# Reordering the opening of an attention + mixer kernel: earlier loads, decay rows moved on chip, the first batch ahead of the mixers

## Chip, cores, metric

One core of a Trainium2 chip. The metric is device time of one execution in microseconds (us), lower is better; medians over several executions are given. TensorE (PE in the profile) multiplies, ACT (ScalarE) does exponentials and copies, VectorE (DVE) copies and masks, GpSimd (POOL) issues most loads, SyncE (SP) the others.

Two words are used throughout. The *opening* is what happens before channel mixing of the first token group starts; the *dense part* is everything after that.

## The reference

```python
# q, k, v: (8 batches, 8 heads, 576, 64); s: (8, 8, 576)
scores = q @ k.T / sqrt(64)
cum    = cumsum(max(s, 0))
scores = where(causal, -1e9, scores + min(-(cum[:, None] - cum[None, :]), 0))
x      = softmax(scores) @ v                    # heads side by side: (8, 576, 512)
u      = x + (x.T @ U @ V).T                    # sequence mixing, rank 32
out    = u + relu(u @ w_ch1) @ w_ch2            # channel mixing, 512 -> 2048 -> 512
```

## The kernel before

Attention goes by pairs of heads, four pairs per batch, 32 in all. One pair is three generators: `transposes` (TensorE turns q and k, VectorE copies them into a slot, and the decay rows, that is the cumulative sums in parts, are added to the slot by DMA), `scores` (matmuls of 68 rows, exponentials on ACT, masking on VectorE) and `values`. After each batch comes `seqmix`, then one group of 512 tokens of `chanmix` is queued as *filler*: each `yield` of the attention lets the filler do one step (four matmuls of 512 columns).

```python
    # ... decay rows: computed on VectorE for all heads, written to HBM
    nc.sync.dma_start(out=rows_hbm.rearrange("r n c s -> n r c s"), in_=rows)
    # ... identity, masks, memsets on POOL, then the loads, all issued by POOL:
    load_qk(0, 4)                  # q, k of batch 0 in four pieces each
    load_v(0)

    def transposes(n):
        b, hp = divmod(n, PB)      # PB = 4 pairs per batch
        slot = slots[n % NSLOT]
        nc.sync.dma_start(out=slot[D:KA, :, 0 : 2 * S],
                          in_=rows_hbm[:, ds(2 * n, 2)].rearrange("r n c s -> r n (c s)"))
        for hh in range(2):
            ...                    # 8 transposes on TensorE, 2 copies on VectorE
            yield                  # 2 yields;  scores: 4 yields, values: 2 yields

    def chanmix(g):                # 32 yields in all
        for nf in range(NF):       # 16 steps, 4 matmuls each
            ...
            yield
        for i in range(4):         # 16 steps, 4 matmuls each
            ...

    fill = []
    def step_fill():
        while fill:
            if next(fill[0], fill) is not fill:
                return
            fill.pop(0)

    def run(gen):
        for _ in gen:
            step_fill()

    drain(transposes(0))
    load_weights()                 # U, V, w1, w2: 8 MB read, 4 MB in bf16
    for n in range(NP + 1):        # NP = 32 pairs
        b, hp = divmod(n, PB)
        if hp == 0 and b + 1 < B:
            load_qk(b + 1, 1)
            load_v(b + 1)
        if n + 1 < NP:
            run(transposes(n + 1))
        if n < NP:
            run(scores(n))
        if n > 0:
            run(values(n - 1))
            if n % PB == 0:
                run(seqmix(b - 1))
                fill.append(chanmix(b - 1))
```

The softmax here doesn't subtract the row's maximum and nothing guards it: scores larger than these inputs give would overflow.

## Time and profile before

| | us |
|---|---|
| time, median (range) | 430.1 (429.5 to 431.3) |
| span of the profiled execution | 429.4 |
| first score matmul | 25.0 |
| sequence mixing of batch 0 starts | 64.2 |
| first channel-mixing matmul of group 0 / of group 1 | 69.9 / 112.4 |

This is the busy time by stretch. The columns are the stretch in us, its length, then busy us (and instructions) of PE, PE weight loads, DVE, ACT, POOL, then the granted clock, the DMA share (the time of all packets over that of 16 engines, so it can exceed 1) and GB/s.

```profile
20.00:30.00 10.00, 4.86 (x44) 3.75 (x45) 1.10 (x4) 3.64 (x8) 7.47 (x9) 1.00 1.74 182
30.00:40.00 10.00, 10.00 (x116) 8.48 (x115) 9.82 (x22) 7.39 (x16) 0.70 (x1) 1.00 1.17 206
40.00:50.00 10.00, 1.14 (x10) 0.58 (x8) 1.23 (x4) 2.46 (x6) 0.83 (x1) 0.68 1.64 191
50.00:60.00 10.00, 6.96 (x92) 6.03 (x93) 5.80 (x10) 1.68 (x4) 3.49 (x4) 0.50 3.26 107
...
70.00:80.00 10.00, 10.00 (x94) 5.43 (x93) 6.80 (x12) 5.38 (x9) 3.48 (x5) 1.00 2.28 71
```

TensorE is the limit from 70 us on (10.00 of 10 us), and it is idle for most of 40 to 50 us. The clock column of the first 40 us is not to be trusted: the durations there are those of half rate (the prediction explains how to see it).

These are TensorE's waits in the first 70 us (what it waited for, total us, times, longest):

```profile
PE pwork L173 <- DMA q_sd<-in_q_dram: 18.4, 3, 9.1
PE pscore L193 <- DMA slot_121<-rows_hbm: 9.8, 1, 9.8
PE pwork L173 <- DMA k_sd<-in_k_dram: 5.2, 3, 1.9
```

18.4 us went into waiting for q, 9.8 for the decay rows of pair 0 that came back from HBM, 5.2 for k. And this is the timeline of TensorE just before sequence mixing of batch 0 (start, duration, line, output and operands, count). Slots go round in threes, so slot_122 and slot_123 here are pairs 4 and 5, which belong to batch 1:

```profile
57.14 1.51 PE L193 MATMUL pscore<-slot_122 68*128 68x128 bf16 x9 [0.75 <-DVE slot_122 L178]
...
59.29 1.52 PE L193 MATMUL pscore<-slot_122 68*128 68x128 bf16 x9
...
61.45 2.91 PE L193 MATMUL pscore<-slot_123 68*128 68x128 bf16 x18
64.16 2.34 PE L269 MATMUL pwork<-x_sb,U_sb 128*128 128x512 bf16 x5
```

### The profile page before, as it was taken

To read this page: it belongs to the slowest core of one execution; us is meant where nothing else is said; L and a number is where in the kernel's file an instruction comes from. 1 tells how busy PE (TensorE), PEld (TensorE's weight loads), DVE (VectorE), ACT (ScalarE), POOL (GpSimd) and SP (SyncE) were. 2 spreads that over 40 slices of the span, in tenths; PEclk is the share of its full clock that TensorE was granted. 3 is DMA by queue.
4 is the path that set the end of the run, shared out by engine and by line. 5 is a ranking of instruction groups with operands and counts; after the bars stand their busy time and mean duration, and the time that the engine had idled before them with its cause. 6 is when DMAs were issued, how large, how long until landed. Compare 5 with 4: busy or idle time off the path is not lost.

```text
span 429.4 us, 8600 instructions
## 1 busy us (share of the span) xinstructions
PE 390.8 (91%) x3608; PEld 229.5 (53%) x3608; DVE 232.9 (54%) x451; ACT 191.4 (45%) x369; POOL 60.4 (14%) x83
## 2 busy tenths in 40 slices
PE   0168289999999999999999999999999999999996
PEld 0156265556555655555565555655565565444443
DVE  7538186566856675567556755685667535101001
ACT  1057053743475347534753375337533760440620
POOL 9750134100310031003100310000000000000000
PEclk9999558999999999999999999999999999999999
DMA  3999999841944193419351925100010001101001
GB/s 53 179 194 206 164 106 125 70 82 52 79 59 84 53 82 51 90 52 81 44 100 52 81 38 103 54 26 4 21 58 27 2 3 49 49 2 73 25 26 73
DMA packets 59351, 29.76 MB, mean 69 GB/s; under 512 B 42320, under 2 KB 53616, under 8 KB 59312
## 3 DMA queue, kind: packets, MB, share of 16 engines
q0 software_dynamic: 53392, 18.44, 51.5%
q1 hardware_dynamic: 5920, 10.77, 7.1%
q8 instruction: 28, 0.46, 0.5%
q14 instruction: 11, 0.09, 0.1%
HBM read 37.58 MB, written 10.03 MB: 111 GB/s over the span
## 4 chain that ended last, share of the span: by engine, by line
PE 85%; DMA 9%; POOL 3%; DVE 1%; issue 1%; POOLq 0%
PE pwork L331 29%; PE pwork L344 29%; PE pscore L193 10%; DMA k_sd<-in_k_dram 7%; PE pwork L246 6%; PE pwork L173 3%; PE pwork L269 2%; DMA v_slot_91<-in_v_dram 2%; PE pwork L355 2%; PE pwork L282 2%; PE pwork L290 2%; POOL k_sd L112 1%; POOL v_slot_91 L120 1%; POOL q_sd L112 1%; DVE uT L298 0%
## 5 line engine op out<-in xcount | busy, mean ns | idle before, releaser
L344 PE MATMUL pwork<-w_sb,hT 128*128 128x512 bf16 x576 | 143.8, 379 | 0.0
L331 PE MATMUL pwork<-uT,w_sb 128*128 128x512 bf16 x576 | 140.5, 379 | 0.2 <-DVE uT L298 0.2
L338 ACT ACTIVATE hT<-pwork 128x512 bf16<-128x512 f32 x144 | 87.6, 608 | 77.8 <-PE pwork L331 77.3
L331 PEld LDWEIGHTS <-w_sb 128*128 128x128 bf16 x576 | 51.1, 98 | 46.9 <-issue 0.3
L344 PEld LDWEIGHTS <-hT 128*128 128x128 bf16 x576 | 50.2, 98 | 42.6
L364 DVE COPY o_sb<-pwork 128x512 f32<-128x512 f32 x36 | 24.9, 692 | 71.1 <-PE pwork L355 71.1
L204 ACT ACTIVATE pT_127<-pscore 128x512 bf16<-128x512 f32 x32 | 19.3, 602 | 74.9 <-PE pscore L193 74.9
L255 DVE RECIPROCAL rec<-pwork 128x5 f32<-128x5 f32 x64 | 12.1, 193 | 60.8 <-PE pwork L246 60.6
L204 ACT ACTIVATE pT_128<-pscore 128x512 bf16<-128x512 f32 x32 | 19.1, 597 | 53.1 <-PE pscore L193 53.0
L178 DVE COPY slot_122<-pwork 64x576 bf16<-64x576 bf16 x44 | 35.2, 800 | 5.4 <-PE pwork L173 4.7
L178 DVE COPY slot_121<-pwork 64x576 bf16<-64x576 bf16 x44 | 35.1, 799 | 3.2 <-PE pwork L173 2.5
L173 PE MATMUL pwork<-identity,q_sd 72*128 72x72 bf16 x256 | 19.9, 206 | 18.6 <-DMA q_sd<-in_q_dram 18.4
L193 PE MATMUL pscore<-slot_121 68*128 68x128 bf16 (+4 forms) x198 | 24.5, 255 | 9.9 <-DMA slot_121<-rows_hbm 9.8
L178 DVE COPY slot_123<-pwork 64x576 bf16<-64x576 bf16 x40 | 32.0, 801 | 2.3 <-PE pwork L173 1.6
L173 PEld LDWEIGHTS <-q_sd 72*128 72x128 bf16 x256 | 16.8, 104 | 29.5 <-DMA q_sd<-in_q_dram 18.8
L256 DVE TENSOR_TENSOR x_sb<-pwork,rec 128x320 bf16<-128x320 f32 x64 | 31.2, 491 | 2.0
L205 DVE TENSOR_TENSOR pT_127<-pT_127,keep 128x512 bf16<-128x512 bf16 x32 | 13.1, 413 | 25.9 <-ACT pT_127 L204 25.9
L193 PE MATMUL pscore<-slot_122 68*128 68x128 bf16 (+4 forms) x198 | 25.3, 259 | 0.9 <-DVE slot_122 L178 0.7
L193 PEld LDWEIGHTS <-slot_121 68*128 68x128 bf16 x198 | 15.4, 104 | 19.3 <-issue 10.8
L173 PE MATMUL pwork<-identity,k_sd 72*128 72x72 bf16 x256 | 19.6, 208 | 5.2 <-DMA k_sd<-in_k_dram 5.2
L246 PEld LDWEIGHTS <-pT_127 128*128 128x128 bf16 x480 | 20.5, 102 | 6.9 <-issue 0.2
L246 PEld LDWEIGHTS <-pT_128 128*128 128x128 bf16 x480 | 20.4, 102 | 7.0
(79 smaller groups left out, 399.0 us busy)
## 6 DMA issues: line engine op xcount, KB each, us to landing
out_dram<-o_sb SPq DMA_DIRECT2D x36, 256.0 KB
w_sb<-in_moe_w_ch_dram POOLq DMA_DIRECT2D x2, 2048.0 KB, 19.8
q_sd<-in_q_dram POOLq DMA_DIRECT2D x7, 576.0 KB, 7.6
k_sd<-in_k_dram POOLq DMA_DIRECT2D x7, 576.0 KB, 10.7
v_slot_91<-in_v_dram POOLq DMA_DIRECT2D x12, 128.0 KB, 8.1
v_slot_94<-in_v_dram POOLq DMA_DIRECT2D x12, 128.0 KB, 5.7
v_slot_97<-in_v_dram POOLq DMA_DIRECT2D x8, 128.0 KB, 9.1
q_sd<-in_q_dram POOLq DMA_DIRECT2D x4, 144.0 KB, 5.1
```

The costliest lines, as they stand in the source:

```text
L173: nc.tensor.transpose(tp[:, c, t2, :], src[:, h, ds(t2 * 128, 128)], identity[:TP, :TP])
L178: nc.vector.tensor_copy(dst[:, :, :, :, par], tp[par * D : par * D + D].rearrange("p c t m -> p c m t"),)
L193: nc.tensor.matmul(dst, lhsT=kT[:, ds(j * 128, 128)], rhs=qT[:, lo:hi], start=True, stop=True,)
L204: nc.scalar.activation(pT[:, hh, 0:512], diag, EXP, scale=scale)
L205: nc.vector.tensor_tensor(pT[:, hh, 0:512], pT[:, hh, 0:512], keep.rearrange("p a b -> p (a b)"), op=ALU.min)
L246: nc.tensor.matmul(po[:, i, :], lhsT=pT[:, hh, ds(place(j, i), 128)], rhs=vt[:, j, h, :], start=(j == 0), stop=(j == i), skip_group_check= ...
L255: nc.vector.reciprocal(rec, po[:, :, D : D + 1])
L256: nc.vector.tensor_tensor(x_sb[:, :, ds(h * D, D)], po[:, :, 0:D], rec.to_broadcast([128, 5, D]), op=ALU.mult,)
L331: nc.tensor.matmul(f1, lhsT=w1_sb[:, kt, ds(nf * 128, 128)], rhs=uT[:, kt, ds(g * 512, 512)], start=(kt == 0), stop=(kt == 3),)
L338: nc.scalar.activation(hT[:, nf, :], f1, RELU)
L344: nc.tensor.matmul(f2, lhsT=hT[:, nf, ds(i * 128, 128)], rhs=w2_sb[:, nf, :], start=(nf == 0), stop=False, skip_group_check=True,)
L364: nc.vector.tensor_copy(o_sb, f2)
```

## The change

Its intent: issue the first loads at once; move the decay rows of batch 0 inside SBUF and send only those of the other batches through HBM; finish attention of batch 0 before any mixing; put q and k of batch 1 between the two weight matrices; keep TensorE's clock up with filler matmuls. The core of the diff:

```diff
-    load_qk(0, 4)                                # behind memsets, in the middle of the setup
+    alloc_qk(0)
+    load_qk(0, 0, 2)                             # first thing on POOL
     identity = consts.tile([128, 128], BF16)
     make_identity(nc, identity)
+    load_qk(0, 2, 2)
+    load_qk(0, 4, 4)
 ...
+    for n in range(PB):                          # rows of batch 0: SBUF to SBUF
+        for hh in range(2):
+            nc.sync.dma_start(
+                out=slots[n][D:KA, hh, 0 : 2 * S],
+                in_=rows[2 * n + hh : 2 * n + hh + 1].rearrange("n r c s -> n r (c s)"),
+            )
 ...
+    nc.gpsimd.dma_start(out=w1_sb, in_=...)      # weights around q, k of batch 1
+    alloc_qk(1)
+    load_qk(1, 0, H)
+    nc.gpsimd.dma_start(out=w2_sb, in_=...)
+    load_v(1)
 ...
-    NSLOT = 3
+    NSLOT = 5
-                nc.vector.tensor_copy(           # slot copies
+                copy = nc.scalar.copy if n < 2 else nc.vector.tensor_copy
 ...
-    drain(transposes(0))
-    load_weights()
-    for n in range(NP + 1):
+    spin(8)                                      # useless 512-column matmuls
+    for n in range(PB):
+        for _ in transposes(n):
+            spin(1)
+    for n in range(PB):
+        drain(scores(n))
+        if n > 0:
+            drain(values(n - 1))
+    drain(values(PB - 1))
+    drain(seqmix(0))
+    fill.append(chanmix(0))
+    fill_with(4)                                 # four filler steps at once
+    run(transposes(PB))
+    for n in range(PB, NP + 1):
         ...
-        if n > 0:
+        if n > PB:
             run(values(n - 1))
```

Memsets also moved from POOL to VectorE, and one decay row is computed on ACT.

More of the change, by code (lines that the diff above doesn't have):

```diff
@@ L59, in pwork, with alloc_qk, load_qk @@
         return ps_w.tile([128, 512], FP32, tag="w", name="pwork")
-    early = work.tile([128, NF, 512], BF16, tag="hT", name="hT").rearrange("p a b -> p (a b)")
-    s_sb = early[:BH, 8 * S : 10 * S].bitcast(FP32)
+    s_early = work.tile([128, NF, 512], BF16, tag="hT", name="hT").rearrange("p a b -> p (a b)")
+    s_sb = s_early[:BH, 8 * S : 10 * S].bitcast(FP32)
+    cum = s_early[:BH, 10 * S : 12 * S].bitcast(FP32)
+    rows = s_early[:BH, : 8 * S].rearrange("p (r c s) -> p r c s", r=4, c=2)
     nc.sync.dma_start(out=s_sb, in_=s.rearrange("b h s -> (b h) s"))
-    nc.vector.tensor_scalar(s_sb, s_sb, 0.0, 1.0 / scale, op0=ALU.max, op1=ALU.mult)
-    cum = early[:BH, 10 * S : 12 * S].bitcast(FP32)
-    nc.vector.tensor_tensor_scan(cum, s_sb, s_sb, 0.0, op0=ALU.add, op1=ALU.max)
-    rows = early[:BH, : 8 * S].rearrange("p (r c s) -> p r c s", r=4, c=2)
-    nc.gpsimd.memset(rows[:, 0:3, 0, :], 1.0)
-    nc.gpsimd.memset(rows[:, 3, 1, :], 1.0)
-    rest = s_sb
-    nc.vector.tensor_scalar_mul(rows[:, 3, 0, :], cum, -1.0)
-    nc.vector.tensor_copy(rows[:, 0, 1, :], cum)
-    nc.vector.tensor_sub(rest, cum, rows[:, 0, 1, :])
-    nc.vector.tensor_copy(rows[:, 1, 1, :], rest)
-    nc.vector.tensor_sub(rest, rest, rows[:, 1, 1, :])
-    nc.vector.tensor_copy(rows[:, 2, 1, :], rest)
-    rows_hbm = nc.dram_tensor("rows_hbm", (4, BH, 2, S), BF16, kind="Internal").ap()
-    nc.sync.dma_start(out=rows_hbm.rearrange("r n c s -> n r c s"), in_=rows)
+    q_t, k_t = {}, {}
+    def alloc_qk(b):
+        q_t[b] = loads.tile([TP, H, TT * D], BF16, tag="q_sd", name="q_sd")
+        k_t[b] = loads.tile([TP, H, TT * D], BF16, tag="k_sd", name="k_sd")
+    def load_qk(b, h, n):
+        for dst, src in ((q_t[b], q), (k_t[b], k)):
+            nc.gpsimd.dma_start(
+                out=dst[:, ds(h, n), :],
+                in_=src[b, ds(h, n)].rearrange("h (p t) d -> p h (t d)", p=TP),
+            )
+    alloc_qk(0)
+    load_qk(0, 0, 2)
     identity = consts.tile([128, 128], BF16)
     make_identity(nc, identity)
+    load_qk(0, 2, 2)
+    load_qk(0, 4, 4)
     keep = consts.tile([128, 4, 128], BF16)
@@ L95, with spin @@
     )
-    q_t, k_t = {}, {}
+    PW = 1664
+    pTs = [consts.tile([128, 2, PW], BF16, name=f"pT{i}") for i in range(2)]
+    nc.vector.memset(pTs[1][:, 0, 0:640], 1.0)
+    nc.vector.memset(rows[:, 0:3, 0, :], 1.0)
+    nc.vector.memset(rows[:, 3, 1, :], 1.0)
+    for pT in pTs:
+        nc.vector.memset(pT[:, :, 1600:], 1.0)
+    NSLOT = 5
+    SK = 5 * 128
+    slots = [consts.tile([128, 2, S + SK], BF16, name=f"slot{i}") for i in range(NSLOT)]
+    for slot in slots:
+        nc.vector.memset(slot[:KA, :, 2 * S :], 0.0)
+    def spin(n):
+        for _ in range(n):
+            nc.tensor.matmul(
+                pscore(),
+                lhsT=pTs[1][:, 0, 512:640],
+                rhs=pTs[1][:, 0, 0:512],
+                start=True,
+                stop=True,
+            )
+    nc.vector.tensor_scalar(s_sb, s_sb, 0.0, 1.0 / scale, op0=ALU.max, op1=ALU.mult)
+    nc.vector.tensor_tensor_scan(cum, s_sb, s_sb, 0.0, op0=ALU.add, op1=ALU.max)
+    rest = s_sb
+    nc.scalar.mul(rows[:, 3, 0, :], cum, -1.0)
+    nc.vector.tensor_copy(rows[:, 0, 1, :], cum)
+    nc.vector.tensor_sub(rest, cum, rows[:, 0, 1, :])
+    nc.vector.tensor_copy(rows[:, 1, 1, :], rest)
+    nc.vector.tensor_sub(rows[:, 2, 1, :], rest, rows[:, 1, 1, :])
+    for n in range(PB):
[3 more added lines that the diff above has]
+                in_=rows[2 * n + hh : 2 * n + hh + 1].rearrange("n r c s -> n r (c s)"),
+            )
+    rows_hbm = nc.dram_tensor("rows_hbm", (4, BH, 2, S), BF16, kind="Internal").ap()
+    nc.sync.dma_start(
+        out=rows_hbm[:, ds(2 * PB, BH - 2 * PB)].rearrange("r n c s -> n r c s"),
+        in_=rows[2 * PB :],
+    )
     v_slots = []
@@ L101 @@
         vt = consts.tile([128, 5, H, D + 1], BF16, name=f"v_slot{i}")
-        nc.gpsimd.memset(vt[:, :, :, D : D + 1], 1.0)
-        nc.gpsimd.memset(vt[64:, 4, :, :], 0.0)
+        nc.vector.memset(vt[:, :, :, D : D + 1], 1.0)
+        nc.vector.memset(vt[64:, 4, :, :], 0.0)
         v_slots.append(vt)
-    def load_qk(b, cuts):
-        q_t[b] = loads.tile([TP, H, TT * D], BF16, tag="q_sd", name="q_sd")
-        k_t[b] = loads.tile([TP, H, TT * D], BF16, tag="k_sd", name="k_sd")
-        n = H // cuts
-        for c in range(cuts):
-            for dst, src in ((q_t[b], q), (k_t[b], k)):
-                nc.gpsimd.dma_start(
-                    out=dst[:, ds(c * n, n), :],
-                    in_=src[b, ds(c * n, n)].rearrange("h (p t) d -> p h (t d)", p=TP),
-                )
     def load_v(b):
@@ L126, in load_v @@
         )
-    load_qk(0, 4)
     load_v(0)
-    w1_sb = consts.tile([128, 4, FF], BF16)
-    w2_sb = consts.tile([128, NF, DM], BF16)
     U_sb = consts.tile([128, 5, 128], BF16)
@@ L135 @@
     nc.vector.memset(V_sb, 0.0)
-    def load_weights():
-        nc.gpsimd.dma_start(
-            out=U_sb[:, :4, :R], in_=moe_U[:512].rearrange("(kt kp) r -> kp kt r", kp=128)
-        )
-        nc.gpsimd.dma_start(out=U_sb[:64, 4, :R], in_=moe_U[512:576])
-        nc.gpsimd.dma_start(out=V_sb[:R], in_=moe_V)
-        nc.gpsimd.dma_start(out=w1_sb, in_=moe_w_ch1.rearrange("(kt kp) n -> kp kt n", kp=128))
-        nc.gpsimd.dma_start(out=w2_sb, in_=moe_w_ch2.rearrange("(kt kp) n -> kp kt n", kp=128))
-    NSLOT = 3
-    SK = 5 * 128
-    slots = [consts.tile([128, 2, S + SK], BF16, name=f"slot{i}") for i in range(NSLOT)]
-    for slot in slots:
-        nc.vector.memset(slot[:KA, :, 2 * S :], 0.0)
-    PW = 1664
-    pTs = [consts.tile([128, 2, PW], BF16, name=f"pT{i}") for i in range(2)]
-    for pT in pTs:
-        nc.vector.memset(pT[:, :, 1600:], 1.0)
+    nc.gpsimd.dma_start(
+        out=U_sb[:, :4, :R], in_=moe_U[:512].rearrange("(kt kp) r -> kp kt r", kp=128)
+    )
+    nc.gpsimd.dma_start(out=U_sb[:64, 4, :R], in_=moe_U[512:576])
+    nc.gpsimd.dma_start(out=V_sb[:R], in_=moe_V)
+    w1_sb = consts.tile([128, 4, FF], BF16)
+    w2_sb = consts.tile([128, NF, DM], BF16)
+    nc.gpsimd.dma_start(out=w1_sb, in_=moe_w_ch1.rearrange("(kt kp) n -> kp kt n", kp=128))
+    alloc_qk(1)
+    load_qk(1, 0, H)
+    nc.gpsimd.dma_start(out=w2_sb, in_=moe_w_ch2.rearrange("(kt kp) n -> kp kt n", kp=128))
+    load_v(1)
     uT = consts.tile([128, 4, B * S], BF16)
@@ L164, in transposes @@
         slot = slots[n % NSLOT]
-        nc.sync.dma_start(out=slot[D:KA, :, 0 : 2 * S], in_=rows_hbm[:, ds(2 * n, 2)].rearrange("r n c s -> r n (c s)"))
+        if b > 0:
+            nc.sync.dma_start(
+                out=slot[D:KA, :, 0 : 2 * S],
+                in_=rows_hbm[:, ds(2 * n, 2)].rearrange("r n c s -> r n (c s)"),
+            )
         for hh in range(2):
@@ L177, in transposes @@
             for par in range(2):
-                nc.vector.tensor_copy(
+                copy = nc.scalar.copy if n < 2 else nc.vector.tensor_copy
+                copy(
                     dst[:, :, :, :, par],
@@ L383, in drain, with fill_with @@
             pass
-    drain(transposes(0))
-    load_weights()
-    for n in range(NP + 1):
+    def fill_with(n):
+        for _ in range(n):
+            step_fill()
+    spin(8)
[12 more added lines that the diff above has]
+    for n in range(PB, NP + 1):
         b, hp = divmod(n, PB)
         if hp == 0 and b + 1 < B:
-            load_qk(b + 1, 1)
+            alloc_qk(b + 1)
+            load_qk(b + 1, 0, H)
             load_v(b + 1)
@@ L395 @@
             run(scores(n))
-        if n > 0:
+        if n > PB:
             run(values(n - 1))
-            if n % PB == 0:
+            if hp == 0:
                 run(seqmix(b - 1))
```

## The prediction

> **What bounds the kernel now.** From about 70 us on, TensorE: the table of busy time by stretch has it 100% busy from 70 to 400 us. The timeline gives 43.3 us per batch (four head pairs at about 2.8 us: transposes 0.5, scores 1.4, values 0.9; mixing over the sequence about 3.5; one group of channel mixing 28.7), and two groups, 57 us, at the end. The change leaves that alone. Of the first 70 us TensorE is busy 35.
>
> The groups and the chain of waits show three losses in this opening.
> 1. POOL issues the first q load only at 4.6 us, behind memsets; q and k of batch 0 land from 8.1 to about 19.3 us.
> 2. The decay rows go to HBM (10.2) and come back (issued 18.4); scores wait for them 9.8 us and start at 25.0.
> 3. Transposes of batch 1 stand before the last values of batch 0, and q, k of batch 1 queue behind all weights (landing about 35.0 and 46.4): q lands at 50.3, k at 55.0. TensorE idles 9.1 + 1.9 us. Sequence mixing of batch 0 runs 64.2 to 69.2; then the dense part starts.
>
> TensorE is also slow until 66 us: 512-column matmuls start 0.43 us apart at 64 to 66 us, 0.216 later. This agrees with the Trainium skill, "TensorE: Matmul & The Clock Gate", Part 1 (half rate until a window of about 3.4 us was busy). The clock row's 1.0 before 40 us can't be right: 72-column transposes took 254 ns there, 192 later.
>
> **What the change does.** The dense part (69.2 to 429.4, 360 us) stays; its start moves. Added to it are transposes of pairs 4 and 5 and scores of 4, done earlier before: 2 x 0.5 + 1.4 = 2.4 us. Estimated new start:
> - First q issue at 0.8 us; last k of batch 0 lands at about 15.
> - Rows are ready at about 9; direct moves land at 13 to 17, no longer limiting.
> - All 32 transposes of the last two pairs stand before scores(0), with fillers: 3.5 us at half rate. Scores start at about 18.
> - Four pairs of scores and values: about 4.5 us each at half rate (ACT's limit about 3.5). Until about 37.
> - Last normalisation 1 us, sequence mixing 5 us at half rate: ends at about 42.
> - Loads, 3.8 us earlier and reordered: first weight at 31, q and k of batch 1 at 40, second weight at 51, v of batch 1 at 60.5. Only the last, needed at about 61, may cost 0 to 2 us.
>
> 42 + 2.4 + 360 = 404 us: 26 less than before, nearly all on the critical path. The fillers (16 x 0.2 to 0.43 us) lie mostly in waits. I expect that they warm the clock for a few us, and that it falls back while TensorE waits for heads 4 to 7, until the sequence mixing. If it stays warm, about 6 us less.
>
> **Prediction: 404 us, 397 to 412. Faster by over 2%: 0.96; within 2%: 0.03; slower: 0.01.**
>
> **Signs.** First channel-mixing matmul at 41 to 44 us (before 69.9); scores(0) at 16 to 19; no TensorE wait over 2 us after 20 us; period still 43.3; row moves no longer among the waits. Clock: 65-column matmuls of batch 0 at 245 ns (cold) or 193 (warm).
>
> **What would make it wrong.** Row moves or q, k slowed by sharing the DMA engines; the order of VectorE's work (copies of pairs 2 and 3, 3.2 us each, before the first masking) delaying values(0); first weight or q, k of batch 1 later than 43, v of batch 1 later than 62; or a warm clock.

## More of the kernel before

The tile framework decides at build time in which order each engine issues its instructions; the program text is a preference only.

## The result, and the profile after

| | before | after | predicted |
|---|---|---|---|
| time, median (range), us | 430.1 (429.5 to 431.3) | 413.5 (412.2 to 416.0) | 404 (397 to 412) |
| span of the profiled execution | 429.4 | 412.1 | |
| first score matmul | 25.0 | 19.0 | 16 to 19 |
| sequence mixing of batch 0 starts | 64.2 | 40.0 | about 37 to 38 |
| first channel-mixing matmul of group 0 | 69.9 | 43.8 | 41 to 44 |
| from there to the first of group 1 | 42.6 | 51.8 | 45.0 |
| from there to the end of the span | 317.0 | 316.5 | 317.0 |

The ratio is 0.962, 95% interval 0.957 to 0.967. Ratios are computed as the mean time of one kernel's fast runs over the mean of the other's fast runs of the same rounds, so they are not quite the ratio of the medians quoted. The predicted 45.0 is the 42.6 of before plus the prediction's 2.4.

The kernel is 4% faster, but the time lies above the predicted range. The table says where the missing part is: the dense part begins nearly when it should, the last 316 us are unchanged, and the stretch between them is 6.8 us too long. The busy time by stretch after:

```profile
10.00:20.00 10.00, 1.00 (x14) 1.03 (x15) 2.17 (x6) 1.93 (x3) 7.18 (x11) 0.53 2.19 151
20.00:30.00 10.00, 8.68 (x85) 6.79 (x83) 6.23 (x9) 9.64 (x19) 3.38 (x4) 0.50 1.07 231
30.00:40.00 10.00, 8.67 (x138) 7.25 (x137) 8.22 (x28) 6.37 (x14) 0.70 (x1) 0.77 1.45 169
...
70.00:80.00 10.00, 10.00 (x105) 6.01 (x103) 6.55 (x14) 3.35 (x8) 2.46 (x4) 1.00 1.62 142
80.00:90.00 10.00, 8.85 (x136) 6.59 (x135) 8.86 (x22) 8.28 (x18) 2.82 (x4) 0.96 0.71 126
90.00:100.00 10.00, 9.61 (x71) 5.03 (x70) 7.49 (x13) 3.60 (x8) 1.42 (x2) 0.87 0.75 48
```

Before, TensorE was full from 70 to 400 us. Now there is a dip at 80 to 100 us, with a clock below 1. This is TensorE's timeline through it (slots now go round in fives: slot_97, 98, 99 are pairs 7, 8, 9; L374 is channel mixing's second half, L223 scores, L276 values, L299 sequence mixing, L361 channel mixing's first half):

```profile
80.90 1.03 PE L374 MATMUL pwork<-w_sb,hT 128*128 128x512 bf16 x4
81.76 0.39 PE L385 MATMUL pwork<-identity,uT 128*128 128x128 bf16 x4
81.99 0.85 PE L223 MATMUL pscore<-slot_97 68*128 68x128 bf16 x9
...
84.11 0.89 PE L223 MATMUL pscore<-slot_98 68*128 68x128 bf16 x10
...
86.84 0.49 PE L223 MATMUL pscore<-slot_99 68*128 68x128 bf16 x5
88.10 0.86 PE L223 MATMUL pscore<-slot_99 68*128 68x64 bf16 x9 [0.77 <-DVE slot_99 L208]
89.27 1.07 PE L223 MATMUL pscore<-slot_99 68*128 68x448 bf16 x4 [0.30 <-ACT pT_89 L243]
90.14 2.34 PE L299 MATMUL pwork<-x_sb,U_sb 128*128 128x512 bf16 x5
...
95.62 0.59 PE L361 MATMUL pwork<-uT,w_sb 128*128 128x512 bf16 x2 [0.18 <-DVE uT L328]
```

The last filler is at 81.76; from 81.99 to 95.62 TensorE has attention and sequence mixing alone. It waits for VectorE's copies and for ACT (brackets), and the five 512-column matmuls of sequence mixing take 2.34 us, where they took 1.24 at full rate in the other batches.

The opening after, same view. L118 are the useless matmuls:

```profile
1.66 6.37 PE L118 MATMUL pscore<-pT_89 128*128 128x512 bf16 x16 [1.66 <-DVE pT_89 L103]
...
8.38 0.43 PE L202 MATMUL pwork<-identity,q_sd 72*128 72x72 bf16 x8
19.00 0.59 PE L223 MATMUL pscore<-slot_95 68*128 68x128 bf16 x4 [10.19 <-DMA slot_95<-hT]
19.37 0.69 PE L202 MATMUL pwork<-identity,k_sd 72*128 72x72 bf16 x8
...
21.26 0.91 PE L202 MATMUL pwork<-identity,q_sd 72*128 72x72 bf16 x12
...
23.59 1.16 PE L202 MATMUL pwork<-identity,k_sd 72*128 72x72 bf16 x16
```

All 16 useless matmuls ran together, and four score matmuls of pair 0 stand in TensorE's order before 40 of the 64 transposes of batch 0. They waited 10.2 us for the decay rows, and the transposes waited behind them.

### The profile page after: what moved, and what is told of

It reads as the page before. It is cut to its first block, busy times and chain, and to the rows that moved or that the text cites. A ratio compares the mean times of both kernels' runs of the same rounds, so it can differ in the third digit from the quotient of the medians.

```text
span 412.1 us, 8636 instructions
## 1 busy us (share of the span) xinstructions
PE 391.6 (95%) x3624; PEld 227.0 (55%) x3624; DVE 228.5 (55%) x452; ACT 197.8 (48%) x378; POOL 55.2 (13%) x73
## 4 chain that ended last, share of the span: by engine, by line
PE 91%; ACT 3%; DVE 2%; DMA 2%; issue 1%; ACTq 0%
PE pwork L361 30%; PE pwork L374 30%; PE pscore L223 11%; PE pwork L276 7%; PE pwork L202 4%; PE pwork L299 2%; PE pwork L385 2%; DMA slot_95<-hT 2%; PE pwork L320 2%; PE pscore L118 2%; PE pwork L312 1%; DVE uT L328 1%; DVE slot_99 L208 1%; ACT slot_96 L208 1%; ACT slot_95 L208 1%
## 5 line engine op out<-in xcount | busy, mean ns | idle before, releaser
L374 PE MATMUL pwork<-w_sb,hT 128*128 128x512 bf16 x576 | 143.8, 379 | 0.0
L361 PE MATMUL pwork<-uT,w_sb 128*128 128x512 bf16 x576 | 140.5, 379 | 0.4 <-DVE uT L328 0.4
L361 PEld LDWEIGHTS <-w_sb 128*128 128x128 bf16 x576 | 51.1, 98 | 47.7 <-issue 0.9
L374 PEld LDWEIGHTS <-hT 128*128 128x128 bf16 x576 | 50.2, 98 | 42.7
L234 ACT ACTIVATE pT_89<-pscore 128x512 bf16<-128x512 f32 x32 | 19.2, 600 | 49.3 <-PE pscore L223 49.3
L234 ACT ACTIVATE pT_88<-pscore 128x512 bf16<-128x512 f32 x32 | 19.3, 604 | 42.4 <-PE pscore L223 42.4
L285 DVE RECIPROCAL rec<-pwork 128x5 f32<-128x5 f32 x64 | 12.2, 194 | 49.1 <-PE pwork L276 48.9
L223 PE MATMUL pscore<-slot_95 68*128 68x128 bf16 (+4 forms) x126 | 15.6, 255 | 10.2 <-DMA slot_95<-hT 10.2
L276 PEld LDWEIGHTS <-pT_88 128*128 128x128 bf16 x480 | 20.1, 100 | 6.7 <-issue 0.2
L276 PEld LDWEIGHTS <-pT_89 128*128 128x128 bf16 x480 | 19.8, 100 | 7.1 <-issue 0.2
L243 ACT ACTIVATE pT_88<-pscore 128x512 bf16<-128x512 f32 x32 | 19.6, 612 | 7.5 <-PE pscore L223 6.2
L328 DVE CAST uT<-pwork 128x512 bf16<-128x512 f32 x32 | 20.1, 683 | 5.2 <-PE pwork L320 5.2
L243 ACT ACTIVATE pT_89<-pscore 128x512 bf16<-128x512 f32 x32 | 19.3, 602 | 6.7 <-PE pscore L223 6.6
L208 DVE COPY slot_97<-pwork 64x576 bf16<-64x576 bf16 x24 | 19.2, 800 | 4.5 <-PE pwork L202 4.1
L208 DVE COPY slot_99<-pwork 64x576 bf16<-64x576 bf16 x24 | 19.2, 799 | 3.8 <-PE pwork L202 3.4
L208 DVE COPY slot_96<-pwork 64x576 bf16<-64x576 bf16 x24 | 19.2, 800 | 2.3 <-PE pwork L202 2.0
L202 PE MATMUL pwork<-identity,q_sd 72*128 72x72 bf16 x256 | 18.7, 198 | 1.4 <-ACT slot_96 L208 1.2
```

Of the source, the lines that this page charges most:

```text
L202: nc.tensor.transpose(tp[:, c, t2, :], src[:, h, ds(t2 * 128, 128)], identity[:TP, :TP])
L208: copy(dst[:, :, :, :, par], tp[par * D : par * D + D].rearrange("p c t m -> p c m t"),)
L223: nc.tensor.matmul(dst, lhsT=kT[:, ds(j * 128, 128)], rhs=qT[:, lo:hi], start=True, stop=True,)
L234: nc.scalar.activation(pT[:, hh, 0:512], diag, EXP, scale=scale)
L243: nc.scalar.activation(pT[:, hh, 512:1024], far, EXP, scale=scale)
L276: nc.tensor.matmul(po[:, i, :], lhsT=pT[:, hh, ds(place(j, i), 128)], rhs=vt[:, j, h, :], start=(j == 0), stop=(j == i), skip_group_check= ...
```

## The experiments

Twelve kernels were run, each correct. "Start" is the first channel-mixing matmul of group 0 and "stretch" the time from there to the first of group 1, both from one profiled execution. "Ratio" is against the kernel before in the same rounds.

| run | one line | median us | ratio (95%) | first score | start | stretch |
|---|---|---|---|---|---|---|
| after | | 413.5 | 0.962 (0.957 to 0.967) | 19.0 | 43.8 | 51.8 |
| e1_pace | fillers spread over batch 1 | 410.7 | 0.953 (0.949 to 0.956) | 18.7 | 43.4 | 47.8 |
| e2_fill0 | no filler steps at once | 413.9 | 0.960 (0.956 to 0.964) | 19.8 | 45.7 | 51.6 |
| e3_fill12 | 12 filler steps at once | 417.0 | 0.966 (0.963 to 0.970) | 18.6 | 43.9 | 53.6 |
| e4_gapspin | useless matmuls in the dip | 413.4 | 0.959 (0.956 to 0.963) | 19.4 | 44.1 | 51.0 |
| e5_nospin | no useless matmuls in the opening | 414.8 | 0.963 (0.960 to 0.965) | 19.4 | 44.7 | 51.9 |
| e6_order | transposes before scores | 411.7 | 0.956 (0.952 to 0.960) | 19.1 | 40.6 | 51.8 |
| e7_latev | v of batch 0 after the row moves | 413.5 | 0.959 (0.956 to 0.962) | 12.5 | 41.3 | 54.5 |
| e8_rowshbm | rows through HBM again | 415.1 | 0.964 (0.962 to 0.966) | 24.3 | 44.9 | 52.0 |
| e9_wfirst | second weight before q, k of batch 1 | 420.4 | 0.972 (0.966 to 0.979) | 19.6 | 44.7 | 59.1 |
| e10_half | e1 + e6 + half of w1 before v | 407.6 | 0.943 (0.940 to 0.946) | 16.5 | 39.6 | 49.4 |
| e11_warm | e1 + e6 + useless matmuls in attention | 407.7 | 0.943 (0.939 to 0.948) | 21.1 | 40.4 | 48.9 |
| e12_v1 | e10 + v of batch 1 before w2 | 405.9 | 0.942 (0.939 to 0.944) | 16.2 | 39.1 | 47.8 |

### The missing filler: e1 to e4

My theory was that fillers run out. Before, batch 1 had after sequence mixing of batch 0 exactly 8 yields for each of pairs 5 to 8, 32 in all, and channel mixing has 32 steps. After, the program runs four steps at once, then transposes(4), transposes(5) and scores(4) with fillers, so 4 + 8 slots are served that before were not there, and the last 12 slots of batch 1 find the queue empty. The rivals were late loads and the clock.

**e1_pace**

```diff
+    slot_no = [0]
+    SLOTS, STEPS = 40, 28
+
     def run(gen):
         for _ in gen:
+            i = slot_no[0]
+            slot_no[0] += 1
+            if i < SLOTS and (i + 1) * STEPS // SLOTS == i * STEPS // SLOTS:
+                continue
             step_fill()
```

> Same work, same first four filler steps after the first sequence mixing; the other 28 steps of channel mixing of batch 0 are spread over the 40 slots of batch 1 (7 of 10) instead of one per slot until they run out. Theory A (batch 1 has 44 slots for 32 filler steps since the change, before it had exactly 32; the last 12 slots run uncovered, limited by the exchange between TensorE, ACT and VectorE and with a falling clock): first channel-mixing matmul of group 0 to that of group 1 shrinks from 51.8 to about 45 us, time 413.4 -> about 407. Rival B (the loss in batch 1 comes from late loads: v of batch 1, decay rows, or q and k of batch 2): the waits stay and move, 413 within 1.5 us. Rival C (only the clock of the later part): no change of the distance, under 1 us.

The stretch fell from 51.8 to 47.8 us and the ratio from 0.962 to 0.953, worth 3.8 us of 430. The dip is gone; this is the end of batch 1 in its timeline (L374 and L385 are fillers):

```profile
82.37 0.85 PE L223 MATMUL pscore<-slot 68*128 68x128 bf16 x9
83.28 0.81 PE L374 MATMUL pwork<-w_sb,hT 128*128 128x512 bf16 x3
83.93 0.61 PE L276 MATMUL pwork<-v_slot,pT 128*128 128x65 bf16 x15
84.38 1.03 PE L374 MATMUL pwork<-w_sb,hT 128*128 128x512 bf16 x4
...
86.57 0.39 PE L385 MATMUL pwork<-identity,uT 128*128 128x128 bf16 x4
86.79 1.03 PE L299 MATMUL pwork<-x_sb,U_sb 128*128 128x512 bf16 x4
```

Only the placing of the steps was edited: no load and no work was added or removed. Late loads are no rival for this dip either: after 20 us no wait of TensorE in after is for a DMA. Theory A is shown for the greater part, but 45 us was expected and 47.8 measured, so a second term was still missing. Counting the matmuls of the stretch gives it. These are groups of TensorE in the stretch, line, shapes and count (then busy us, mean ns of one, idle us before them); first the kernel before, from 69.85 to 112.44 us:

```profile
L193 PE MATMUL pscore<-slot_121 68*128 68x128 bf16 (+4 forms) x27 | 3.2, 240 | 0.0
...
L173 PE MATMUL pwork<-identity,q_sd 72*128 72x72 bf16 x32 | 2.4, 195 | 0.0
...
L193 PE MATMUL pscore<-slot_122 68*128 68x128 bf16 (+4 forms) x18 | 2.0, 240 | 0.0
L193 PE MATMUL pscore<-slot_123 68*128 68x128 bf16 (+4 forms) x18 | 2.0, 240 | 0.0
```

Then after, from 43.81 to 95.62 us:

```profile
L223 PE MATMUL pscore<-slot_99 68*128 68x128 bf16 (+4 forms) x36 | 4.5, 254 | 1.1 <-DVE slot_99 L208 0.8 <-ACT pT_89 L243 0.3
L202 PE MATMUL pwork<-identity,q_sd 72*128 72x72 bf16 x52 | 3.8, 195 | 0.2 <-DVE uT L328 0.2
...
L223 PE MATMUL pscore<-slot_95 68*128 68x128 bf16 (+4 forms) x18 | 2.0, 240 | 0.0
L223 PE MATMUL pscore<-slot_96 68*128 68x128 bf16 (+4 forms) x18 | 2.0, 239 | 0.0
L223 PE MATMUL pscore<-slot_98 68*128 68x128 bf16 (+4 forms) x18 | 2.0, 239 | 0.1
L223 PE MATMUL pscore<-slot_97 68*128 68x128 bf16 (+4 forms) x18 | 1.9, 239 | 0.0
```

Score matmuls went from 27 + 18 + 18 = 63 to 36 + 4 x 18 = 108, and transposes from 64 to 104 (twice the q line, as k has the same count). A pair has 18 and 16 of them and costs 1.38 and 0.52 us at full rate, so 45 and 40 more are 2.5 pairs each, 3.45 + 1.30 = 4.75 us. I had predicted two pairs of transposes and one of scores, 2.4 us.

Which half pairs these are is in the timeline of the kernel before. Its 27 matmuls of slot_121 (which holds pairs 6 and 9 in this stretch) are all 18 of pair 6 and, from 109.80 us on, 9 of the 18 of pair 9:

```profile
80.19 0.42 PE L193 MATMUL pscore<-slot_121 68*128 68x128 bf16 x5
...
109.80 0.28 PE L193 MATMUL pscore<-slot_121 68*128 68x128 bf16 x2
```

So the scores of pairs 4 and 5 came into the stretch from in front of it, and half of pair 9 from behind it (after does all 18 of them before group 1). The transposes all came from in front: pairs 4 and 5 and the first head of pair 6.

At full rate the stretch should take 42.6 + 4.75 = 47.3 us; after's took 51.8, so 4.5 us are left, which I put down to the uncovered slots. In e1 the stretch has 99 score matmuls, 9 fewer, as half of pair 9 is done behind it again, like before (0.7 us: the rest of the span is 317.2 us, in after 316.5). So of the 4.0 us that the stretch lost, 3.3 are gained by the pacing, and of the 4.5 about 1.1 stayed.

**e2_fill0 and e3_fill12** change one number.

```diff
-    fill_with(4)
+    fill_with(0)      # e2_fill0
+    fill_with(12)     # e3_fill12
```

> No filler steps right after the first sequence mixing: 8 uncovered slots at the end of batch 1 instead of 12. Theory A: the loss of about 6.8 us falls by a third, 413.4 -> about 411. If the four steps were needed to cover the wait for q and k of batch 1 (they land at about 40, before the sequence mixing ends at 43.8), it becomes slower by up to 3 us instead. Rival B: no change.

> 12 filler steps right after the first sequence mixing: 20 uncovered slots instead of 12. Theory A: 413.4 -> about 418 (0.57 us for each slot). Rival B (late loads): the same or faster, since batch 1 asks for its data later by 7 us.

e2 gained 0.002 in the ratio, 0.8 us, well inside its interval: a miss. Its start is 1.9 us later: sequence mixing itself began 1.3 us later in this build, and four transposes of pair 4 now stand before the first filler step. No wait for q or k appears. e3 lost 0.005, 2 us, where 4.6 was expected; its stretch is 1.7 us longer. Both have the expected direction and less than half of the size, and neither interval is clear of after's. The slot price of 0.57 us was 6.8 / 12 and contained the 2.35 us of miscounted work; 4.5 / 12 is 0.37. Even so the loss is not shown to go by the number of slots. Rival B of e3, that batch 1 profits from asking later, is not seen.

**e4_gapspin**

```diff
     def run(gen):
         for _ in gen:
+            slot_no[0] += 1
+            if not fill and slot_no[0] <= 40:
+                for _ in range(1):
+                    nc.tensor.matmul(
+                        pwork(), lhsT=w1_sb[:, 0, 0:128], rhs=w1_sb[:, 0, 0:512], start=True, stop=True
+                    )
             step_fill()
```

> After's order, but each uncovered slot of batch 1 gets one useless 512-column matmul (12 in all, 0.22 us each at full rate). If the loss of the uncovered stretch is mostly the clock falling to half rate, 413.4 -> 411 to 412 and the sequence-mixing matmuls of batch 1 start 0.22 instead of 0.43 us apart. If it is mostly the missing useful work (ACT's and VectorE's pace), 413.5 to 415: filler without use fills time but saves none.

The clock stayed up (granted 1.00 from 80 to 100 us, 0.96 and 0.87 in after; the four recorded sequence-mixing matmuls took 1.25 us), yet the stretch is 51.0, and the ratio is 0.003 lower, inside the interval. The 11 useless matmuls that the trace has cost 11 x 0.22 = 2.4 us of TensorE time. By these two profiles a full clock is worth at least the 0.8 us that the stretch fell and at most 0.8 + 2.4 = 3.2 us; how the 4.5 us divide between clock and waits stays open. What useful filler does (e1), useless filler does not.

### The opening: e5 to e8

**e5_nospin** removes `spin(8)` and the `spin(1)` after each half pair of transposes.

> After's kernel without any of the 16 filler matmuls of the opening. In after they all ran together from 1.7 to 8.0 us, the clock was full for the first transposes, and by 19 us (10 us without work) it was half again. Theory: they buy nothing, 413.4 within 1.5 us; scores(0) still wait for the row moves until about 19, the 65-column matmuls of the first pair take about 245 ns as in after. Rival: the warm-up is worth something because transposes are done earlier: 415 to 417 without it.

0.963 against 0.962: no difference is seen. The start is 0.9 us later in the trace; by this pair of profiles the useless matmuls bring no more than that. They warm the clock for transposes that then have to wait anyway.

**e6_order** fixes TensorE's order, which the scheduler had chosen.

```diff
-    for n in range(PB):
-        drain(scores(n))
+    with tc.issue_after(last_t[0].ins):     # the last transpose of batch 0
+        drain(scores(0))
+    for n in range(PB):
         if n > 0:
+            drain(scores(n))
             drain(values(n - 1))
```

> All 64 transposes of batch 0 are placed before the first score matmul in TensorE's order (in after, four score matmuls of pair 0 stood before 40 of them and held them up from 8.8 to 19.0 us, though q and k had landed by about 13). Theory: scores(0) still start at 19, but then nothing of pairs 1 to 3 is in the way, and VectorE's copies of pairs 2 and 3 (3.2 us each) are done by about 20: the first sequence mixing starts at about 36 to 37.5 instead of 40.0, time 413.4 -> about 410. Rival: the four pairs are bound by ACT after 19 us anyway: within 1 us.

The first score matmul still waits until 19.1, but the start moved from 43.8 to 40.6 and the stretch is the same 51.8. The ratio fell by 0.0055, 2.4 us; the intervals overlap a little. So the misplaced score matmuls cost 2 to 3 us. What the rest of the wait costs this run can't tell, as the wait for the rows is still there (3.9 us, until 19.1); e7 and e10 shorten it.

**e7_latev** lets POOL copy a word of pair 0's rows before it issues any load after q and k of batch 0.

```diff
+    gate_i = nc.gpsimd.tensor_copy(gate[D:KA, :], slots[0][D:KA, 1, 0:8])
+    with tc.issue_after(gate_i.ins):
         load_v(0)
         ...                       # U, V, w1, q and k of batch 1, w2, v of batch 1
```

> POOL issues the v loads of batch 0 and everything after them only when the decay rows of pair 0 have landed. In after the moves of 9 KB took 7.7 us (issued 11.2, seen by TensorE 18.9) while v was loading in 128-byte packets. If sharing the DMA engines makes them slow, they take 2 to 4 us now, scores(0) start at 13.5 to 15.5, and the time falls by 2 to 4 us unless the later loads (all about 3 us later) become the limit. If the form of the move itself is slow (one source partition), it takes 7 us still and the time rises by up to 3 us.

The rows, issued at 10.4, were used at 12.5: 2.1 us instead of 7.7. Nothing in the moves was changed, only what shared the DMA engines with them. The first score matmul came 6.5 us earlier, the start 2.5 us, and the time not at all (0.959, inside the interval), since the stretch grew by 2.7. TensorE's waits:

```profile
PE pwork L279 <- DMA v_slot<-in_v_dram: 4.9, 3, 1.7
PE pscore L226 <- DMA slot<-hT: 4.5, 1, 4.5
```

4.9 us for v are new: two of the three waits (3.3 us) are for v of batch 0, in the opening, and one (1.7 us) for v of batch 1, in the stretch. The gain was handed back to later loads. The Trainium skill, "DMA: Bandwidth & Descriptors", section "Queues, rings and completion order", says that each DMA engine goes round the queues that have work, a packet at a time. That this makes a small move slow fits the 7.7 us beside v's packets; the page gives no figure for it.

**e8_rowshbm** deletes the SBUF-to-SBUF moves and writes and reads the rows of batch 0 through HBM, as before.

> The decay rows of batch 0 go through HBM again, as before the change; all else as after. Theory: scores(0) start at 24 to 26 (before: 25.0, with the write issued at 10.2; here about 11.2) instead of 19.0, and as nothing else is late by then, the time rises by 5 to 6.5 us, to about 419.

The first score matmul went to 24.3 as expected, but the start only to 44.9, and the ratio rose by 0.002, 1 us: a miss. In this build TensorE does its transposes before it waits, so waiting longer cost little. The 5.3 us that the direct move saves were almost wholly lost again in after to the order of TensorE. With the order mended (e6) the same direct move starts channel mixing 4.3 us earlier than e8.

### The order of the loads: e9

```diff
+    nc.gpsimd.dma_start(out=w2_sb, in_=...)
     alloc_qk(1)
     load_qk(1, 0, H)
-    nc.gpsimd.dma_start(out=w2_sb, in_=...)
     load_v(1)
```

> After's kernel with one line moved: the second weight matrix is loaded ahead of q and k of batch 1, as before the change. Theory: q and k then land about 10 us later (near 47 and 51 instead of 38.9 and 40.1), TensorE waits for them 3 to 5 us at the transposes of pair 4 (due at 47.4), and 3 to 5 us are lost: 416.5 to 418.5. If the load order has no part in the gain: within 1 us of 413.5.

```profile
PE pwork L202 <- DMA q_sd<-in_q_dram: 3.9, 1, 3.9
```

The wait for q of batch 1 is back, 3.9 us, inside the 3 to 5 expected. The stretch grew by 7.3 us and the ratio by 0.0105, 4.5 us (by the medians 7; this call's intervals are wide, and the profiled execution, 422.0 us, was one of its slower ones). Part of what the wait doesn't explain is the clock, which fell during it (granted 0.50 from 54 to 56 us). So q and k between the weights is a real part of the gain.

### Putting it together: e10 to e12

**e10_half** has e1's pacing, e6's order, and `w1_sb[:, 0:2]` loaded ahead of v of batch 0, the rest in the old place.

> Three edits on after: fillers paced as in e1 (-3.8 us), transposes of batch 0 placed ahead of scores(0) as in e6 (-2.4 us), and half of the first weight matrix loaded ahead of v of batch 0, so that the row moves share the DMA engines with large packets instead of v's 128-byte ones. Without the last edit the first two should give about 407.5 (ratio 0.947) if they add. If large packets leave the row moves quick (2 to 3 us, as without any load beside them), scores(0) start at 13.5 to 15 and the first channel mixing at 37 to 38.5: 404 to 406. If any load slows them alike, scores(0) start at 18 to 20 and v comes 4.6 us later: 407 to 409.

It took 407.6 us. The rows came at 16.5, 5.4 us after their issue: between both guesses, large packets slow the moves as well, only less. The start is 39.6, later than the 37 to 38.5 of the better case, and the stretch is 49.4, as v now comes too late (two waits, 1.4 us, in the opening, and one of 1.3 us in the stretch):

```profile
PE pwork L284 <- DMA v_slot<-in_v_dram: 2.7, 3, 1.3
```

**e11_warm** has pacing and order, and adds fillers without use:

```diff
+    with tc.issue_after(last_t[0].ins):
+        warm(14, pscore)                 # 512 columns, identity times the mask
+    with tc.issue_after(last_t[0].ins):
+        for _ in scores(0):
+            warm(1, pwork)               # likewise in scores(1) to scores(3)
```

> Fillers paced and transposes ahead as in e10, loads as in after, and useless matmuls of 512 columns: 14 ahead of scores(0) and one after each of the 16 half-steps of the scores of batch 0. Tests the prediction's 'if the clock stays warm, about 6 us less'. If so, the 65-column matmuls of the first pair take 193 ns instead of 245 and the first sequence mixing starts at 34 to 35 instead of 36.8, for about 405.5; more than that is not to be had, as ACT needs about 3.5 us per pair. If the clock falls all the same, the fillers cost their own 16 x 0.43 us in part: 409 to 412.

The clock was up from about 20 us: all values matmuls of batch 0 ran at the short duration, in after 60 of 120, as its clock rose only at about 34.5 us. First e11, then after, groups of 65-column matmuls between 10 and 36 us:

```profile
L277 PE MATMUL pwork<-v_slot,pT 128*128 128x65 bf16 x120 | 4.6, 194 | 0.1
```

```profile
L276 PE MATMUL pwork<-v_slot_121,pT_89 128*128 128x65 bf16 x30 | 2.2, 245 | 0.0
```

194 ns against 245. Sequence mixing nevertheless started at 36.7, against 36.8 in e6. The 14 fillers ran into the time of the scores, which began 2.0 us later (21.1), and the warm attention won 2.1 us (15.6 us from first score to sequence mixing instead of 17.7). So in attention a warm clock, together with the matmuls that keep it warm, is worth 2 us. ACT holds it: it was busy 11.8 of the 12 us from 22 to 34 us, in e6 10.0. The prediction's "about 6 us less" counted sequence mixing at half rate too, but that ran at full rate already in after (3.8 us instead of 5). Both together are 3.3 us, about half of the 6.

**e12_v1** is e10 with `load_v(1)` ahead of the second weight.

> e10's kernel with v of batch 1 loaded ahead of the second weight matrix. In e10 everything came earlier and TensorE then waited 1.3 us for v of batch 1 (landing 51 to 58), so first to second channel mixing took 49.4 us instead of e1's 47.8. Theory (loads of batch 1 are the next limit, and only their order is wrong, since the second weight is not needed before about 60): the waits for v go, the distance returns to 47.5 to 48.2, 406 us, ratio 0.939 to 0.942. If the second weight now comes too late (it would land at about 58), a wait appears at the second half of channel mixing: 408 to 410.

405.9 us, ratio 0.942; the wait for v is gone and the stretch is 47.8. This kernel has the lowest median (its interval overlaps those of e10 and e11), 25 us under the kernel before and 8 under the change as given.

## Why the prediction was wrong

The direction and most of the mechanism held; the size was 26 us predicted, 16.6 measured. Working it out on the profiled spans: I had the first channel-mixing matmul at about 42.6 (sequence mixing ends at 42, and it follows 0.6 us later, as before). After it come the stretch, 42.6 us before plus my 2.4, and the rest, 317.0: the span is 404.6. Measured:

| term | predicted | measured | difference |
|---|---|---|---|
| first channel-mixing matmul | 42.6 | 43.8 | +1.2 |
| first stretch | 42.6 + 2.4 = 45.0 | 51.8 | +6.8 |
| the rest | 317.0 | 316.5 | -0.5 |
| span | 404.6 | 412.1 | +7.5 |

The rest of the 9.4 us between 404 and 413.4: the sum had been rounded down by 0.6, and the median time lies 1.3 above this span.

- **The step that failed** is "The dense part (69.2 to 429.4, 360 us) stays; its start moves. Added to it are ... 2 x 0.5 + 1.4 = 2.4 us." It failed twice. The work added to the stretch was 45 score matmuls and 40 transposes, 4.75 us: the kernel before had done also the scores of pair 5 and half of the transposes of pair 6 ahead of the point that I moved (1.38 + 0.26 us), and half of the scores of pair 9 came in from behind (0.69 us, which the rest gives back for the most part: its -0.5). I had read the order from the program, not from the trace. And the dense part did not stay dense: 32 filler steps had been matched to 32 slots, and with 44 slots the last 12 ran uncovered, which cost another 4.5 us. e1 shows it for the greater part: spreading the same steps took 4.0 us off the stretch, 3.3 of them for good. The prediction nowhere sets slots against filler steps.
- **The opening** was right in its sum (41 to 44 predicted, 43.8 measured), by errors that cancelled. q and k landed earlier than I put them (the last k at 12.7, not 15), the row moves later (18.9, not 13 to 17), and the order of TensorE tied the transposes to the rows, which I had not foreseen (e6: 2 to 3 us). "Row moves no longer among the waits" was wrong: they are the longest wait there is, 10.2 us.
- **Loads of batch 1**: right. They came in time, no wait over 2 us after 20 us, and e9 shows what the other order would cost.
- **The clock**: it was warm at 8 us, cold from 19 to past 30, as I expected, with one difference: it was up again at about 34.5 us, before sequence mixing, which took 3.8 us instead of 5. "If it stays warm, about 6 us less" was too much (2.1 us in attention by e11, and 1.2 in sequence mixing that after already had). And the agreement with the Trainium skill that the prediction notes holds for the two rates, not for the window: see the last section.
- **Period 43.3 later, TensorE's busy time about the same**: right (the rest of the span agrees within 0.5 us).
- Still open: how the uncovered loss divides between clock and waits (e4 leaves 0.8 to 3.2 us for the clock), and the 1.1 us that pacing left.

## What to carry to other kernels

When fillers are handed out one per slot, count slots and steps on both sides of a change: moving work to the other side of the filler's start changes the ratio, and the uncovered tail then costs time (here about 4.5 us). Take the work that a change moves from counts in the trace between two fixed marks, not from the program order, as the scheduler may long have moved it. And before saving a wait, check what else on the same engine or the same DMA engines is queued behind it: here 6.5 us saved at the first score matmul (e7) gave nothing, as later loads took them back.

## What the Trainium skill lacked or had wrong

- "TensorE: Matmul & The Clock Gate", Part 1, has full rate after about 3.4 us of sustained work. With matmuls of 512 columns it took about 3 and 4 us here (before: begun at 64.2, up at 67.3 us; e11: 15.8 and 20.1). With attention (score matmuls of 68 rows, values of 65 columns, transposes) it took far longer, though TensorE had no wait over 0.2 us: in after, at work from 23.4 us on, the clock rose at about 34.5 us (65-column matmuls from 243 to 196 ns), and in before, at work from 25.0 us on, only at about 40.0 us (128-column score matmuls from 314 to 219 ns). Part 4 says that transposes do not count as busy in the same way; how much such short matmuls count it doesn't say, and nothing here isolates it.
- The same page, Part 1: the clock falls after an idle window of about 3.4 us; it also tells of a kernel in which short idle stretches between groups of matmuls did it. How little idle is enough it doesn't say. In after it fell at about 89.3 us, when TensorE had been shown busy 1.92 of the 3 us from 87 to 90 us and its longest pause was 0.77 us; one 512-column matmul per slot kept it up (e4).
- "DMA: Bandwidth & Descriptors", section "Queues, rings and completion order", gives the turn-taking of queues but no price for a small transfer beside large ones: the same 9 KB moves were usable 2.1 us after issue when the loads ahead of them had nearly drained (e7), 5.4 with weights (e10), 7.7 with v in 128-byte packets (after).
